# Summing a vector over the partitions: two matmuls replaced by two crossbar turns, in a kernel that TensorE bounds

## The chip, the cores and the metric

One core of one Trainium2 chip. The metric is the device time of one execution in microseconds (us), as the median of several executions. PE is TensorE, DVE is VectorE, ACT is ScalarE, POOL is GpSimd; SP is the queue that issues most of the DMAs.

## The reference, cut to what matters

The program mixes a linear-attention block A and an MLP-mixer block B by a gate. Only the denominator of A matters here:

```python
pq, pk = phi(q), phi(k)                        # [B, H=32, S=2048, Dh=20]
z   = jnp.einsum("bhsd->bhd", pk)              # sum over all 2048 tokens
den = jnp.einsum("bhqd,bhd->bhq", pq, z)[..., None] + 1e-6
o   = num / den
# B: h = gelu(layernorm(x) @ w1); hs = shifted h @ w2; x1 = x + hs
#    b = x1 + gelu(layernorm(x1) @ w3) @ w4
return g * a + (1 - g) * b
```

`z` is one vector of 640 numbers (32 heads of 20). Tokens lie on the 128 partitions, so the sum over tokens has two steps: over the 16 token tiles (elementwise), and over the 128 partitions. Every partition needs the whole vector afterwards, because each multiplies its own `pq` rows with it.

## The kernel before

The first step is a chain of VectorE additions that leaves `zsum` [128, 640] in bf16. The second is the part that changes:

```python
def z_add(t):                                   # VectorE, 15 times; the last writes zsum
    tt(dve, zacc if t < NT - 1 else zsum, pk_tok[:, 0] if t == 1 else zacc, pk_tok[:, t], ALU.add)

def zb_group():                                 # ones^T @ zsum: summed over partitions AND spread to all of them
    b = pair()                                  # two PSUM banks
    mm_group(ps[:, b, 0:512],     [(ones_c[:, 0:128], zsum[:, 0:512])])
    mm_group(ps[:, b + 1, 0:128], [(ones_c[:, 0:128], zsum[:, 512:D])])
    copy(dve, zb[:, :], psf[:, 512 * b:512 * b + D])
...
IT.add("ZB", ("zb",), 0.0, zb_group, deps=[(("z", NT - 1), 1.7), (("w2", 0), 0.0)])

def qn_sum(t):                                  # the reader of zb: VectorE, once for each of 16 tiles
    tt(dve, qprod, pq_tok[:, t + 1], zb, ALU.mult)
    dve(tensor_reduce(dnr[:, 0, sd, :], qprod as 32 heads of 20, ADD))

def t_xn(which, t):                             # "turned tile t": crossbar transpose of a normalised tile, on SP
    sch.dma("sp", xnT[:, :, 128 * t:128 * (t + 1)], xn[:, sx, :], ..., transpose=True)
```

(`...` and shortened arguments mark cuts.) Two facts about the surroundings matter:

- The kernel writes one fixed instruction order for each engine. A small time model inside the program decides that order when the kernel is built; an `IT.add(..., deps=...)` entry is emitted only once its dependencies are done by that model. On the chip each engine works through its list in that order, waiting on semaphores, so a list entry that waits holds up what stands behind it on that engine (turn12_not_held below shows it: VectorE sat idle for 4.74 us before one product, and the W2 sum behind it came 5 us late).
- `xn`, the buffer of normalised tiles, is a ring of three, so tile `t` is normalised only after tile `t - 3` has been turned. Behind the 16 turned tiles of the first norm, SP issues the loads of `w3` and `w4` (2.1 MB each), then the turned tiles of the second norm.

Of the kernel before, what the change touches and what calls it, by code (L numbers as in the profile page):

```python
# [6 lines left out]
F32 = mybir.dt.float32  # L7
ACTF = mybir.ActivationFunctionType
ALU = mybir.AluOpType

S = 2048
D = 640
# [3 lines left out]
NT = S // 128  # L16
NCH = S // 512
KD = D // 128
# [398 lines left out]
def _build(nc, A_x, A_wqkv, A_wo, B_w1, B_w2, B_w3, B_w4, gate_w, out, dbg=None, stop=None):  # L417
    sch = _Sched(nc)
# [37 lines left out]
    pa = Arena(SB_LO, SB_HI - SHARED)  # L456
# [3 lines left out]
    ps = nc.alloc_psum_tensor("ps", [128, 8, 512], F32)  # L460
# [5 lines left out]
    ones_c = pa.alloc("ones_c", [128, 768], BF16)  # L466
# [10 lines left out]
    w2 = pa.alloc("w2", [128, KD, D], BF16)  # L477
# [8 lines left out]
    M_sb = pa.alloc("M_sb", [128, KD, D], BF16)  # L486
    zb = pa.alloc("zb", [128, D], BF16)
    dnr = pa.alloc("dnr", [128, 2, 4, H], F32)
    xn = pa.alloc("xn", [128, 3, D], BF16)
    junk = pa.alloc("junk", [128, 1, D], BF16)  # L490
    qprod = pa.alloc("qprod", [128, D], F32)
    zacc = qprod
    zsum = pa.alloc("zsum", [128, D], BF16)
# [34 lines left out]
    psf = ps[:, :, :].rearrange("p b n -> p (b n)")  # L528
    bank_hold = set()

    def pair():
        best = None
        for k_ in range(4):
            q_ = (bank_rr[0] // 2 + k_) % 4
            tf = 0.0
            ok = True
            for b in (2 * q_, 2 * q_ + 1):
                if b in bank_pend or b in bank_hold:
                    ok = False
                lk = sch.locks.get(b)  # L540
                if lk is not None:
                    tf = max(tf, sch.ev_time.get((lk[1].sem, lk[1].val), 1e18))
            if ok and (best is None or tf < best[0]):
                best = (tf, 2 * q_)
        b = best[1]
        bank_rr[0] = b + 2
        bank_pend.update((b, b + 1))
        return b
# [3 lines left out]
    def slot(name, n):  # L552
        i = slot_ctr.get(name, 0)
        slot_ctr[name] = i + 1
        return i % n

    def nfree(ap):
        n = 1
        for d_ in ap.shape[1:]:
            n *= d_  # L560
        return n

    def in_psum(ap):
        return ap.tensor.name == ps.name

    def act(fn, reads, writes, cost=None):
        if cost is None:
            n = nfree(writes[0])
            cost = max(150.0, 100.0 + 0.833 * n + (70.0 if (reads and in_psum(reads[0])) else 0.0))
            cost += 45.0 * max(0, len(reads) - 1)  # L570
        return sch.op("act", fn, reads, writes, cost=cost)

    def dve(fn, reads, writes, cost=None):
        if cost is None:
            n = nfree(writes[0])
            cost = 65.0 + n / 0.96
        return sch.op("dve", fn, reads, writes, cost=cost)
# [7 lines left out]
    def pe(fn, reads, writes, cost=500.0):  # L585
        for w_ in writes:
            sp_, rl = sch.rects(w_)
            if sp_ == "ps":
                for (_p0, _p1, lo, hi) in rl:
                    for b in range(lo // PS_BANK, (hi - 1) // PS_BANK + 1):  # L590
                        bank_pend.discard(b)
        return sch.op("pe", fn, reads, writes, cost=cost)

    def mm_group(out_ap, pairs, reads_extra=()):
        n = len(pairs)

        def fn(e, out_ap=out_ap, pairs=pairs, n=n):
            ins = None
            for i, (l, r) in enumerate(pairs):
                ins = e.matmul(out_ap, l, r, start=(i == 0), stop=(i == n - 1))  # L600
            return ins
        reads = [a for p in pairs for a in p] + list(reads_extra)
        return pe(fn, reads, [out_ap], cost=n * (max(nfree(pairs[0][1]), 24) * 0.4167 + 2.5))
# [39 lines left out]
    def activation(out_ap, in_ap, func, scale=1.0, bias=0.0, accum=None):  # L643
        rd = [in_ap] + [a for a in (scale, bias) if not isinstance(a, (int, float))]
        wr = [out_ap] + ([accum] if accum is not None else [])
        n = nfree(out_ap)
        cost = max(150.0, 100.0 + 0.833 * n + (70.0 if in_psum(in_ap) else 0.0)) + 45.0 * (len(rd) - 1)
        if accum is not None:
            cost += 91.0
        st_ = ACT_SET.get(func)  # L650
        if st_ is not None and st_ != sch.act_func:
            cost += 1290.0
            sch.act_func = st_
        if accum is not None:
            return act(lambda e: e.activation(out_ap, in_ap, func, bias=bias, scale=scale, accum_out=accum), rd, wr, cost=cost)  # L655
        return act(lambda e: e.activation(out_ap, in_ap, func, bias=bias, scale=scale), rd, wr, cost=cost)  # L656
# [4 lines left out]
    def copy(engf, out_ap, in_ap):  # L661
        cost = None
        if engf is dve and in_ap.dtype == BF16 and out_ap.dtype == BF16:
            cost = 65.0 + nfree(out_ap) / 1.92
        return engf(lambda e: e.tensor_copy(out_ap, in_ap), [in_ap], [out_ap], cost=cost)  # L665
# [90 lines left out]
    def tag_chk(buf, sl, what):  # L756
        assert tags.get((buf, sl)) == what, ("stale ring slot", buf, sl, what, tags.get((buf, sl)))

    IT = _Items()
# [83 lines left out]
    def normalize(which, t, st):  # L843
        sx = slot("xn", 3)
        tag_set("xn", sx, (which, t))
        xn_slots[(which, t)] = sx
        ts(pool, xn[:, sx, :], x_tok[:, t, :], st[:, 6, t:t + 1], st[:, 7, t:t + 1], ALU.mult, ALU.add)

    def t_xn(which, t):
        sx = xn_slots[(which, t)]  # L850
        tag_chk("xn", sx, (which, t))
        sch.dma("sp", xnT[:, :, 128 * t:128 * (t + 1)], xn[:, sx, :], "trn%d" % slot("trn", 4), transpose=True)
# [77 lines left out]
    def stats1(c):  # L930
        ln_chunk_stats(st1, c, lr[:, 4 * c:4 * c + 4, 0:1].rearrange("p t o -> p (t o)"))
        gate_chunk(c)

    for u in range(NT):
        if u % 4 == 0:
            IT.add("S1", ("s1", u // 4), 0.0, lambda u=u: stats1(u // 4), deps=[(("k", u + 3), 1.8)])
        d1 = [(("s1", u // 4), 3.0 + 0.9 * (u % 4))]
        d1.append((("k", 13), 0.0) if u == 0 else (("n1", u - 1), 0.9))
        if u >= 3:
            d1.append((("t1", u - 3), 0.0))  # L940
        IT.add("N1", ("n1", u), 0.0, lambda u=u: normalize(1, u, st1), deps=d1)
        IT.add("T1", ("t1", u), 0.0, lambda u=u: t_xn(1, u), deps=[(("n1", u), 1.1)])
    for u in range(1, NT):
        IT.add("Z", ("z", u), 0.0, lambda u=u: z_add(u), deps=[(("k", NT - 1), 2.0)] if u == 1 else [])
    LAST_EXP = ("k", NT - 1)
# [76 lines left out]
        for j in range(KD):  # L1022
            sch.dma("sp", M_sb[60:68, j, :], Mt[8 * j:8 * j + 8, :], "mt", group_total=KD)

    def zb_group():
        b = pair()
        mm_group(ps[:, b, 0:512], [(ones_c[:, 0:128], zsum[:, 0:512])])
        mm_group(ps[:, b + 1, 0:128], [(ones_c[:, 0:128], zsum[:, 512:D])])
        copy(dve, zb[:, :], psf[:, 512 * b:512 * b + D])

    IT.add("KVF", ("kvt", 1), 0.0, kvt_group, deps=[(("g", KD - 1), 1.0)])
    IT.add("KVF", ("lt", 1), 0.0, lt_evac, deps=[(("kvt", 1), 0.0)])
    IT.add("KVF", ("m", 0), 0.0, m_last, deps=[(("lt", 1), 1.0), (("w1", 2, 2), 0.0)])
    IT.add("KVF", ("m", 1), 0.0, m_first, deps=[(("lt", 1), 1.0), (("w3", 0, 5), 0.0)])
    IT.add("MT", ("mt",), 0.0, m_tail, deps=[(("m", 1), 1.5), (("qt", 2), 0.0)])
    IT.add("ZB", ("zb",), 0.0, zb_group, deps=[(("z", NT - 1), 1.7), (("w2", 0), 0.0)])

    SHIFT = (1, -1, 2, -2)
    PIECES = [[(0, 128, SHIFT[j])] for j in range(4)] + [[(32 * g_, 32 * (g_ + 1), SHIFT[g_]) for g_ in range(4)]]
# [156 lines left out]
    for c in range(NCH):  # L1196
        for j in range(KD):
            deps = [(("t1", u), 0.9) for u in range(4 * c, 4 * c + 4)] if j == 0 else []
# [6 lines left out]
    for t in range(NT):  # L1205
        c = t // 4
        deps = [(("w1", c, KD - 1), GEL)]
# [8 lines left out]
    for u in range(NT):  # L1216
        deps = [(("s2", u // 4), 3.2 + 0.9 * (u % 4))]
# [8 lines left out]
    for c in range(NCH):  # L1226
        for j in range(KFF):
            deps = []
# [4 lines left out]
            if j == 0:  # L1233
                deps = deps0 + [(("t2", u), 0.9) for u in range(4 * c, 4 * c + 4)]
# [11 lines left out]
    for t in range(NT):  # L1246
        deps = [(("zb",), 1.0), (("q", max(t, 2)), 2.0)]
# [12 lines left out]
    for t in range(NT):  # L1260
        c = t // 4
        deps = [(("qt", t), 3.0), (("w4load",), 0.0), (("m", 1), 1.0), (("mt",), 2.5)]
# [29 lines left out]
def bass_gated_mix__linear_attn_block__mixer_s_mlp__prompt_kernel(  # L1292
    nc, A_x, A_wqkv, A_wo, B_x, B_w1, B_w2, B_w3, B_w4, gate_w, out
):
    assert tuple(A_x.shape) == (1, S, D) and tuple(out.shape) == (1, S, D)
    assert tuple(A_wqkv.shape) == (D, 3 * D) and tuple(A_wo.shape) == (D, D)
    assert tuple(B_w1.shape) == (D, D) and tuple(B_w2.shape) == (D, D)
    assert tuple(B_w3.shape) == (D, F) and tuple(B_w4.shape) == (F, D) and tuple(gate_w.shape) == (D,)
    _build(nc, A_x, A_wqkv, A_wo, B_w1, B_w2, B_w3, B_w4, gate_w, out)
# [28 lines left out]
```

## Time and profile before

| what | value | where it is read |
|---|---|---|
| time | 260.59 us (260.18 to 260.70, 3 runs) | run list |
| PE busy | 254.3 of 259.1 us | part 1 of the page |
| chain that ended last | 98% PE | part 4 of the page |
| the two matmuls | 0.27 us | timeline of PE |

Three lines of the page of the kernel before: its first line, PE's line of part 1 (busy us, share, instructions) and the first line of part 4.

```profile
span 259.1 us, 4261 instructions
...
PE 254.3 (98%) x1654; PEld 132.5 (51%) x1685; DVE 152.0 (59%) x288; ACT 106.6 (41%) x216; POOL 93.8 (36%) x151
...
PE 98%; issue 1%; DVE 1%
```

A busy share alone would prove little. The chain says more: followed back from the last instruction, it hardly ever leaves PE. The list of PE's waits from 60 us on says the same: in nearly 200 us PE waits for no other engine.

```profile
engine line waited for: us in total, times, longest us
PE ps L600 <- issue: 0.2, 1, 0.2
PE ps L1167 <- issue: 0.2, 1, 0.2
```

The timeline of PE around the two matmuls (start, length, engine, line, operation, count). A length runs to the modelled end of a pipelined matmul, so lengths overlap; the cost of a group is the distance from its start to the start of the next group.

```profile
82.22 1.24 PE L600 MATMUL ps<-xnT,w 128*128 128x512 bf16 x5
83.30 0.43 PE L600 MATMUL ps<-zsum,ones_c 128*128 128x512 bf16 x2
83.57 1.52 PE L600 MATMUL ps<-w,hsT 128*128 128x512 bf16 x10
```

83.57 - 83.30 = 0.27 us, not the printed 0.43. Another pair of a 512 and a 128 column matmul in the same trace, that of `wq`, has the same distance: one starts at 6.21 us and the next at 6.48 us.

The same stretch on VectorE: the cast that brings `zb` out of PSUM, a W2 sum (L637), then the first product with `zb`.

```profile
82.42 0.82 DVE L637 SCALAR_TENSOR_TENSOR x_tok<-ps,x_tok 128x640 bf16<-128x640 f32 x1 [3.75 <-PE ps L600]
...
83.77 0.82 DVE L665 CAST zb<-ps 128x640 bf16<-128x640 f32 x1 [0.52 <-PE ps L600]
85.13 0.82 DVE L637 SCALAR_TENSOR_TENSOR x_tok<-ps,x_tok 128x640 bf16<-128x640 f32 x1 [0.53 <-PE ps L600]
...
85.88 0.82 DVE L630 TENSOR_TENSOR qprod<-pq_tok,zb 128x640 f32<-128x640 bf16 x1
```

And the SP queue from 72 us on: nine turned tiles with no gap worth naming, the w3 and w4 loads, then, 9 us after the last of those was issued, the first turned tiles of the second norm.

```profile
69.69 13.22 SPq L281 DMA_TRANSPOSE xnT<-xn  x9
82.95 8.14 SPq L285 DMA_DIRECT2D w<-in_B_w_dram  x4
100.15 5.59 SPq L281 DMA_TRANSPOSE xnT<-xn  x4
```

### The profile page before, as it was taken

Reading aid. Unit: us, or ns where it says so; the run is one execution under the profiler, and the core shown is the slowest. Engines: PE = TensorE matmul, PEld = TensorE weight load, DVE = VectorE, ACT = ScalarE, POOL = GpSimd, SP = SyncE. Lnnn points to the kernel's source line nnn. Section 1 sums busy time; section 2 is a strip of 40 time slices with the busy share of each in tenths; the row PEclk is TensorE's granted clock in tenths of the full one; section 3 lists DMA queues with packets and bytes.
Section 4 is the critical chain, followed back from the end, with each engine's and each line's share of the span. In section 5 each row is a group of like instructions: output and inputs, shape, how many; then the busy total and the mean of one; then the engine's idle time right before and its main releaser. Section 6 shows DMA issues by size and latency. Waiting matters only on the chain.

```text
span 259.1 us, 4261 instructions
## 1 busy us (share of the span) xinstructions
PE 254.3 (98%) x1654; PEld 132.5 (51%) x1685; DVE 152.0 (59%) x288; ACT 106.6 (41%) x216; POOL 93.8 (36%) x151
## 2 busy tenths in 40 slices
PE   8999999999999999999999999999999999999996
PEld 4555555544454555554444445554455544455453
DVE  1587877899903799998997407992033410143233
ACT  1496677751365766676854240005500045100000
POOL 4013995969954029666914202320011110021001
DMA  6865998672856992552726640232000020000211
GB/s 181 246 148 137 155 226 156 186 121 50 99 109 124 355 338 47 62 101 52 105 53 122 124 66 0 47 90 67 0 3 0 3 101 0 0 3 1 104 51 51
DMA packets 51406, 25.16 MB, mean 97 GB/s; under 512 B 42766, under 2 KB 49975, under 8 KB 51386
## 3 DMA queue, kind: packets, MB, share of 16 engines
q1 hardware_dynamic: 50000, 21.47, 37.1%
q0 software_dynamic: 1136, 3.28, 5.1%
q8 instruction: 13, 0.21, 0.4%
q10 hardware_dynamic: 250, 0.14, 0.2%
q14 instruction: 7, 0.06, 0.1%
HBM read 12.05 MB, written 2.62 MB: 57 GB/s over the span
## 4 chain that ended last, share of the span: by engine, by line
PE 98%; issue 1%; DVE 1%
PE ps L600 61%; PE ps L1167 22%; PE ps L796 8%; PE ps L889 2%; PE ps L862 1%; PE ps L1079 1%; PE ps L1149 1%; PE ps L890 1%; PE ps L611 1%; DVE x_tok L639 0%; PE ps L969 0%; PE ps L998 0%; DVE xT L665 0%; PE ps L1146 0%
## 5 line engine op out<-in xcount | busy, mean ns | idle before, releaser
L600 PE MATMUL ps<-xnT,w 128*128 128x512 bf16 x348 | 80.4, 379 | 0.7 <-issue 0.2
L1167 PE MATMUL ps<-w,h2T 128*128 128x512 bf16 (+1 forms) x409 | 58.3, 298 | 0.5 <-issue 0.2
L656 ACT ACTIVATE h2T<-ps 128x512 bf16<-128x512 f32 x52 | 30.5, 598 | 67.5 <-PE ps L600 67.5
L600 PEld LDWEIGHTS ps<-xnT,w 128*128 128x128 bf16 x360 | 34.1, 98 | 38.5 <-issue 0.9
L639 DVE SCALAR_TENSOR_TENSOR x_tok<-ps,stg,abx 128x512 bf16<-128x512 f32 (+1 forms) x32 | 17.3, 550 | 61.5 <-PE ps L1167 61.5
L622 POOL TENSOR_SCALAR abx<-x_tok,stg 128x640 f32<-128x640 bf16 x16 | 15.3, 959 | 99.0 <-DVE x_tok L639 94.9
L1167 PEld LDWEIGHTS ps<-w,h2T 128*128 128x128 bf16 x416 | 32.1, 98 | 24.9 <-issue 1.1
L622 POOL TENSOR_SCALAR xn<-x_tok,st 128x640 bf16<-128x640 bf16 x32 | 35.0, 1102 | 14.4 <-DMA xnT<-xn 13.9
L656 ACT ACTIVATE Er<-ps 128x640 bf16<-128x640 f32 x32 | 22.4, 709 | 16.9 <-PE ps L600 8.4
L655 ACT ACTIVATE junk<-x_tok 128x640 bf16<-128x640 bf16 x32 | 23.6, 739 | 3.1 <-DVE x_tok L637 2.6
L656 ACT ACTIVATE hsT<-ps 128x512 bf16<-128x512 f32 (+1 forms) x32 | 18.9, 593 | 13.0 <-PE ps L600 12.7
L600 PE MATMUL ps<-M_sb,pqnT 128*128 128x128 bf16 (+1 forms) x156 | 23.6, 297 | 0.3
L600 PE MATMUL ps<-w,hsT 128*128 128x512 bf16 (+1 forms) x160 | 23.7, 299 | 0.0
L639 DVE SCALAR_TENSOR_TENSOR abx<-ps,stg,abx 128x640 f32<-128x640 f32 x16 | 14.1, 884 | 12.5 <-PE ps L600 11.5
L600 PE MATMUL ps<-wkg,xT 128*128 128x130 bf16 (+1 forms) x138 | 21.1, 298 | 0.1
L600 PE MATMUL ps<-wq,xT 128*128 128x128 bf16 (+1 forms) x128 | 19.7, 298 | 0.1
L600 PEld LDWEIGHTS ps<-w,hsT 128*128 128x128 bf16 x160 | 13.3, 98 | 12.1
L600 PEld LDWEIGHTS ps<-M_sb,pqnT 128*128 128x128 bf16 x160 | 13.2, 98 | 10.8
L796 PE MATMUL ps<-pk_tok,x_tok 128*128 128x512 bf16 x79 | 17.7, 379 | 0.1
L622 DVE TENSOR_SCALAR Er<-Er 128x640 bf16<-128x640 bf16 x32 | 11.8, 368 | 9.4 <-ACT Er L656 9.3
L637 DVE SCALAR_TENSOR_TENSOR x_tok<-ps,x_tok 128x640 bf16<-128x640 f32 x16 | 13.1, 820 | 6.8 <-PE ps L600 5.9
L1108 DVE TENSOR_TENSOR pq_tok<-pq_tok,dnr 128x300 bf16<-128x300 bf16 (+1 forms) x48 | 16.7, 401 | 0.6
(78 smaller groups left out, 228.0 us busy)
## 6 DMA issues: line engine op xcount, KB each, us to landing
w<-in_B_w_dram SPq DMA_DIRECT2D x1, 2160.0 KB, 9.3
w<-in_B_w_dram SPq DMA_DIRECT2D x1, 2080.0 KB, 14.8
out_dram<-x_tok SPq DMA_DIRECT2D x3, 640.0 KB, 3.1
x_tok<-in_A_x_dram SPq DMA_DIRECT2D x2, 640.0 KB, 5.5
w<-in_B_w_dram POOLq DMA_DIRECT2D x8, 160.0 KB, 4.5
x_tok<-in_A_x_dram SPq DMA_DIRECT2D x5, 160.0 KB, 3.0
wq<-in_A_wqkv_dram SPq DMA_DIRECT2D x5, 160.0 KB, 3.9
wkg<-in_A_wqkv_dram SPq DMA_DIRECT2D x5, 160.0 KB, 4.1
```

Of the source, the lines that this page charges most:

```text
L600: ins = e.matmul(out_ap, l, r, start=(i == 0), stop=(i == n - 1))
L611: ins = e.transpose(o, s_, ident[:])
L622: return engf(lambda e: e.tensor_scalar(out_ap, in_ap, s1, s2, op0, op1), rd, [out_ap], cost=cost)
L637: return dve(lambda e: e.scalar_tensor_tensor(out_ap, in0, scalar, in1, op0, op1, accum_out=accum), rd, [out_ap, accum], cost=cost + 70.0)
L639: return dve(lambda e: e.scalar_tensor_tensor(out_ap, in0, scalar, in1, op0, op1), rd, [out_ap], cost=cost)
L655: return act(lambda e: e.activation(out_ap, in_ap, func, bias=bias, scale=scale, accum_out=accum), rd, wr, cost=cost)
L656: return act(lambda e: e.activation(out_ap, in_ap, func, bias=bias, scale=scale), rd, wr, cost=cost)
L796: ins = e.matmul(o, l, r, start=(t0 + q_ == 0), stop=(t0 + q_ == NT - 1))
L862: ins = e.matmul(ps[:, b, 0:n], one[:, 0:128], one[:, 0:n], start=True, stop=True)
L889: e.matmul(ps[:, b, 0:512], l, w[:, k, 0:512], start=(k == 0), stop=(k == KD - 1))
L1108: dve(lambda e, o=o, i0=i0, i1=i1: e.tensor_tensor(o, i0, i1, ALU.mult), [i0, dnr[:, 1, sd, :]], [o], cost=cost)
L1167: ins = e.matmul(o, l, r, start=False, stop=(i == KFF - 1), skip_group_check=(n0 > 0))
```

## The change

Its intent is to take the sum over partitions off PE. A crossbar turn puts the 640 columns of `zsum` on the partitions (five blocks of 128), so VectorE can sum along the free axis. ScalarE spreads each sum over 128 columns, and a second turn brings the vector back, now the same on every partition. So that the second turn is not late, turned tile 12 is held until it is issued.

```diff
+    zc = pa.alloc("zc", [128, KD], F32)
...
-        IT.add("T1", ("t1", u), 0.0, lambda u=u: t_xn(1, u), deps=[(("n1", u), 1.1)])
+        IT.add("T1", ("t1", u), 0.0, lambda u=u: t_xn(1, u), deps=[(("n1", u), 1.1)] + ([(("zb",), 0.0)] if u == 12 else []))
...
-    def zb_group():
-        b = pair()
-        mm_group(ps[:, b, 0:512], [(ones_c[:, 0:128], zsum[:, 0:512])])
-        mm_group(ps[:, b + 1, 0:128], [(ones_c[:, 0:128], zsum[:, 512:D])])
-        copy(dve, zb[:, :], psf[:, 512 * b:512 * b + D])
+    zT = zb[:, :].rearrange("p (k n) -> p k n", n=128)
+    zrep = zsum[:, :].rearrange("p (k n) -> p k n", n=128)
+
+    def z_turn():
+        sch.dma("sp", zT, zsum[:, :], "trz", transpose=True)
+
+    def z_rows():
+        dve(lambda e: e.tensor_reduce(zc[:, :], zT, mybir.AxisListType.X, ALU.add), [zT], [zc[:, :]], cost=820.0)
+        activation(zrep, zc[:, :].unsqueeze(2).to_broadcast([128, KD, 128]), ACTF.Copy)
+
+    def z_back():
+        sch.dma("sp", zT, zsum[:, :], "trz", transpose=True)
...
-    IT.add("ZB", ("zb",), 0.0, zb_group, deps=[(("z", NT - 1), 1.7), (("w2", 0), 0.0)])
+    IT.add("ZB", ("zt",), 0.0, z_turn, deps=[(("z", NT - 1), 1.7), (("t1", 7), 0.0)])
+    IT.add("ZB", ("zr",), 0.0, z_rows, deps=[(("zt",), 2.6), (("kvt", 1), 0.0)])
+    IT.add("ZB", ("zb",), 0.0, z_back, deps=[(("zr",), 1.5)])
```

## The prediction

> **What bounds the kernel now.** TensorE. The page's first part has it 98% busy (254.3 of 259.1 us). The chain that ended last agrees: 98% PE, 1% issue, 1% VectorE. From 70 us on, the list of PE's waits names no other engine, only issue gaps of 0.2 us. So only less PE work, or a new PE wait, moves the time.
>
> **Removed.** Two matmuls (zsum against ones, 512 and 128 columns). In PE's timeline they start at 83.30 and the next group at 83.57 us: 0.27 us, all on the chain. Their PSUM pair and a VectorE cast (0.825 us at 83.77) go too.
>
> **Added.** Two crossbar turns on SP, each as in the trace 1.2-1.3 us of issue and 2.6 us to landing. A VectorE reduction of 640 elements; the one in the trace takes 0.82 us, so VectorE is even. A ScalarE copy, 0.7 us estimated from the 0.70-0.74 us of other 640-element activations; a Copy beside Gelu (M_sb, 125.8 us) needs no table load. [...]
>
> **Moved.**
> - zsum ends at 71.75 us. The first turn goes out beside turned tile 8, at 72-73, landing about 75; tiles 8 to 11 slip 1.3 us. Tile 11 lands about 80.3; its W1 group starts about 86.0: slack over 4 us.
> - Reduction between 75 and 78.5, copy among the gelus about 79-80, way back out about 80, landing about 82.5-83. zb was complete at 84.6, so its first product (85.88) comes at the same time or up to 1.5 us earlier.
> - Turned tile 12 slips from 77.7 to about 81.3; tile 15 waits for xn's ring of three and slips from 81.6 to about 85, landing about 88. Their W1 group starts about 97.3: slack about 9 us.
> - The w3 load slips from 82.95 to about 86.5, landing about 96; first W3 group about 110. The w4 load ends about 3.5 us later, about 102, and may slow the second norm's first turned tiles (issued from 100.15; the fourth lands about 107, needed about 110). It should hold.
> - Gelus about 79-81 slip by up to 0.7 us; PSUM's banks absorb it.
>
> **Sum.** -0.27 us of PE, everything else off the chain: 260.59 - 0.27 = 260.3 us. The order is fixed ahead by the kernel's own model, so a small reorder or other bank assignment can cost or gain a few tenths; before's runs spread 0.5 us. Predicted 260.3 us, range 259.9 to 260.9. Faster by over 2%: 0.01; within 2%: 0.97; slower by over 2%: 0.02.
>
> **What would show it.** Two PE matmuls fewer; PE busy about 0.3 us less between 66 and 100 us; the chain still 98% PE; two more transposes, the second issued about 80 us; zb first read at 84-86 us; tile 15 turned about 85 us.
>
> **What would make it wrong.** (a) A VectorE or ScalarE instruction of the new path placed early in its engine's order and waiting for a turn, so that gelus or W2 sums behind it are late and PE runs out of PSUM banks. (b) The later w4 load colliding with the second norm's turns, so that PE waits at the first W3 group. (c) A changed order of PE groups that exposes another wait, up to about 1 us. (d) An earlier zb or the freed PSUM pair removing gaps; little is to win, as PE has about 0.3 us of them between 70 and 256 us.

## The result, and the profile after

| | before | after |
|---|---|---|
| median of 6 runs | 260.61 us (260.18 to 260.88) | 260.21 us (259.83 to 260.42) |
| ratio | | 0.9987, 95% interval 0.9974 to 0.9999 |

A ratio is the mean time of one kernel's fast runs over that of the other's of the same rounds, so not quite the ratio of the medians. Executions over 1.5% slower than the fastest of the same kernel are left out of the means. The prediction was 260.3 us, range 259.9 to 260.9.

The page of the kernel after, the lines that answer to those above:

```profile
span 259.2 us, 4290 instructions
...
PE 256.2 (99%) x1683; PEld 132.5 (51%) x1683; DVE 151.9 (59%) x288; ACT 107.2 (41%) x217; POOL 93.4 (36%) x151
...
PE 98%; DVE 1%; issue 0%
```

Read carelessly, this page says that nothing was gained: the span grew by 0.1 us, PE is busier and ran more matmuls. None of the three is the work of the change. The trace before has lost matmul records: 1654 stand beside 1685 weight loads, against 1683 beside 1683 in the trace after. The weight loads, 1685 before and 1683 after, show the two that went. The two "issue" waits of the kernel before are likely lost records too: they stand in all five traces that lack about 31 matmul records and in none of the others. The span has another cause. The next two lines are the same matmul of the start-up in PE's timeline, of the kernel before and then of the kernel after:

```profile
5.63 0.38 PE L889 MATMUL ps<-wq,xT 128*128 128x512 bf16 x1
```

```profile
5.69 0.63 PE L890 MATMUL ps<-wq,xT 128*128 128x512 bf16 x1
```

It takes 0.38 us in one and 0.63 us in the other. 0.63 us is what a 512-column matmul takes in turn12_not_held where the granted clock is recorded as 0.50 (four in a row, begun 0.42 us apart, span 1.89 us), so I infer that PE's clock rose later in the execution that was profiled after the change. The clock column of these two traces does not show it: it reads 1.00 from the start in both. Why the two executions differ here is not shown. PE is level in the two traces at 5.4 us and 0.35 us later in the kernel after from 10.8 us to 77 us, so this delay was there before the change had begun.

So the two traces must be compared from a point behind the start-up. I use the place where the chain enters the group that forms kv (line 969 before, 970 after) and the last two VectorE steps, which the chain shows as one piece. From the chain in order of time (start, length, what), before and then after:

```profile
76.62 1.06 PE ps L969 x50
...
256.33 1.08 DVE x_tok L639 x2
```

```profile
76.97 1.06 PE ps L970 x50
...
256.41 1.08 DVE x_tok L640 x2
```

256.33 - 76.62 = 179.71 us before, 256.41 - 76.97 = 179.44 us after: 0.27 us less. I call this number the **fixed stretch**. It is 179.44 us in both traces of the kernel after (the second is the run after_again), while whole runs spread over 0.5 us, so it is the finer instrument. It is still one execution each time, and the kernel before was traced only once.

PE's timeline at the place of the matmuls, after:

```profile
82.57 1.24 PE L601 MATMUL ps<-xnT,w 128*128 128x512 bf16 x5
83.65 1.52 PE L601 MATMUL ps<-w,hsT 128*128 128x512 bf16 x10
```

From group to group it is now 1.08 us (1.35 before). The list of PE's waits from 60 us on is empty. Compared instruction by instruction, PE's order is that of before without the two matmuls. VectorE after:

```profile
77.64 0.82 DVE L1033 TENSOR_REDUCE zc<-zb 128x5 f32<-128x640 bf16 x1 [5.56 <-DMA zb<-zsum]
...
82.77 0.82 DVE L638 SCALAR_TENSOR_TENSOR x_tok<-ps,x_tok 128x640 bf16<-128x640 f32 x1 [3.45 <-PE ps L601]
...
83.52 0.82 DVE L631 TENSOR_TENSOR qprod<-pq_tok,zb 128x640 f32<-128x640 bf16 x1
```

The first product with `zb` now comes directly behind the first W2 sum and ahead of the second, 2.4 us earlier than before. SP after, with the two new turns and the hold:

```profile
74.89 1.27 SPq L281 DMA_TRANSPOSE zb<-zsum  x1
76.21 2.60 SPq L281 DMA_TRANSPOSE xnT<-xn  x2
80.70 1.20 SPq L281 DMA_TRANSPOSE zb<-zsum  x1
81.95 5.58 SPq L281 DMA_TRANSPOSE xnT<-xn  x4
87.57 7.51 SPq L285 DMA_DIRECT2D w<-in_B_w_dram  x4
100.74 5.27 SPq L281 DMA_TRANSPOSE xnT<-xn  x4
```

The queue stands still from 78.8 to 80.7 us (the hold: it waits for ScalarE's copy). The turned tiles 12 to 15 and the w3 and w4 loads go out about 4.5 us later. The second norm's first turns go out 0.6 us later, of which 0.35 us is the start-up.

### The profile page after: what moved, and what is told of

It is laid out like the page before. It is cut to its first block, busy times and chain, and to the rows that moved or that the text cites. A ratio compares the mean times of both kernels' runs of the same rounds, so it can differ in the third digit from the quotient of the medians.

```text
span 259.2 us, 4290 instructions
## 1 busy us (share of the span) xinstructions
PE 256.2 (99%) x1683; PEld 132.5 (51%) x1683; DVE 151.9 (59%) x288; ACT 107.2 (41%) x217; POOL 93.4 (36%) x151
## 4 chain that ended last, share of the span: by engine, by line
PE 98%; DVE 1%; issue 0%
PE ps L601 61%; PE ps L1177 22%; PE ps L797 8%; PE ps L890 2%; PE ps L863 1%; PE ps L1089 1%; PE ps L1159 1%; PE ps L891 1%; PE ps L612 1%; DVE x_tok L640 0%; PE ps L970 0%; PE ps L999 0%; DVE xT L666 0%; PE ps L1156 0%
## 5 line engine op out<-in xcount | busy, mean ns | idle before, releaser
L601 PE MATMUL ps<-xnT,w 128*128 128x512 bf16 x360 | 81.5, 379 | 0.0
L601 PE MATMUL ps<-M_sb,pqnT 128*128 128x512 bf16 (+1 forms) x160 | 24.3, 299 | 0.0
L601 PE MATMUL ps<-wq,xT 128*128 128x512 bf16 (+1 forms) x130 | 19.8, 299 | 0.0
L1118 DVE TENSOR_TENSOR pq_tok<-pq_tok,dnr 128x300 bf16<-128x300 bf16 (+1 forms) x48 | 15.7, 381 | 0.6
L601 PEld LDWEIGHTS ps<-wkg,xT 128*128 128x128 bf16 x140 | 11.4, 97 | 8.4
```

Source lines behind the costliest of these rows:

```text
L601: ins = e.matmul(out_ap, l, r, start=(i == 0), stop=(i == n - 1))
L1118: dve(lambda e, o=o, i0=i0, i1=i1: e.tensor_tensor(o, i0, i1, ALU.mult), [i0, dnr[:, 1, sd, :]], [o], cost=cost)
```

## The experiments

Theory: the gain is PE's own 0.27 us, and everything added lies off the chain. The rivals: the first result was noise; or the gain comes from the earlier `zb`, the missing cast or the freed PSUM pair; or the turns cost something and the removal is worth more. A second question is what the hold on tile 12 is for and how much room there is around it.

The results together; "stretch" is the fixed stretch of the one profiled execution, and "to before" the ratio in the same rounds.

| run | median us (range) | to before (95%) | stretch us |
|---|---|---|---|
| kernel before | 260.33 to 260.61 (medians of its four sets) | 1 | 179.71 |
| kernel after, first result | 260.21 (259.83 to 260.42) | 0.9987 (0.9974 to 0.9999) | 179.44 |
| after_again | 260.52 (260.02 to 260.68) | 0.9993 (0.9981 to 1.0005) | 179.44 |
| turns_and_matmuls | 260.65 (260.12 to 261.09) | 1.0002 (0.9990 to 1.0013) | 179.71 |
| no_matmuls_no_turns | 260.17 (259.70 to 260.68) | 0.9986 (0.9973 to 0.9998) | 179.44 |
| eight_more_pairs | 262.84 (262.62 to 262.95) | 1.0087 (1.0058 to 1.0117) | 181.89 |
| turn12_not_held | 264.80 (264.19 to 266.89) | 1.0168 (1.0142 to 1.0193) | 185.67 |
| hold_tile14 | 260.48 (260.25 to 260.91) | 1.0001 (0.9985 to 1.0017) | 179.65 |
| not_held_late_product | 260.59 (260.39 to 260.69) | 1.0004 (0.9988 to 1.0021) | 179.88 |
| one_dead_turn | 260.29 (259.99 to 260.71) | 0.9993 (0.9978 to 1.0008) | 179.47 |
| two_dead_turns | 262.58 (261.65 to 262.79) | 1.0069 (1.0039 to 1.0099) | 181.31 |
| two_dead_turns_w4_later | 260.16 (259.69 to 260.98) | 0.9990 (0.9968 to 1.0012) | 179.56 |
| five_dead_turns | 273.12 (269.53 to 273.13, its 3 fast runs; a fourth, 273.89, was slow) | 1.0435 (1.0358 to 1.0512) | not taken |

The first four experiments ran on one chip, eight_more_pairs with two_dead_turns and five_dead_turns on a second, the others on a third. All results were correct, except that of no_matmuls_no_turns, which is wrong.

### after_again: is there a gain at all?

No edit.

> The changed kernel itself once more, as the yardstick of this chip. Theory (the gain is the two matmuls taken off TensorE's chain, 0.27 us): about 0.27 us under before, ratio 0.9990. Rival (the first result was noise of the start-up, nothing gained): ratio 1.000.

Measured: ratio 0.9993, and the interval includes 1. The times of this chip alone could not tell 0.27 us from nothing. The fixed stretch could: 179.44 us again. The chain is less steady: on this run's page it is 92% PE and 4% DMA instead of 98% PE, for the same kernel, with the same stretch and again no wait of PE from 60 us on.

### turns_and_matmuls: is it the matmuls?

```diff
+    def dead_pair():
+        b = pair()
+        mm_group(ps[:, b, 0:512], [(ones_c[:, 0:128], w1[:, 0, 0:512])])
+        mm_group(ps[:, b + 1, 0:128], [(ones_c[:, 0:128], w1[:, 0, 512:D])])
...
+    IT.add("DEAD", ("dead",), 0.0, dead_pair, deps=[(("w2", 0), 0.0)])
```

> The changed kernel with a dead pair of matmuls (ones against 512 and 128 columns of a weight, result unread) put back at the old place after the first W2 tile; the turns stay. Theory (only TensorE's own work counts): the gain is gone, level with before, about 260.6 us, ratio 1.000, and 0.27 us over the changed kernel. Rival (the gain is from the earlier zb, from the freed VectorE cast or from the PSUM pair's later eviction): stays at about 260.3, ratio 0.999.

Measured: ratio 1.0002, stretch 179.71 us, that of before to the last digit. The early `zb`, the missing cast and the shorter hold on PSUM are all present here, and nothing is gained. Those rivals fall.

### no_matmuls_no_turns: do the turns cost anything?

```diff
 # on the kernel before; wrong result on purpose
-        b = pair()
-        mm_group(...)
-        mm_group(...)
-        copy(dve, zb[:, :], psf[:, 512 * b:512 * b + D])
+        dve(lambda e: e.tensor_copy(zb[:, :], zsum[:, :]), [zsum[:, :]], [zb[:, :]], cost=731.0)
```

> The kernel before with the two matmuls dropped and zb copied by VectorE straight from zsum: wrong result on purpose, no turns at all. TensorE's order is that of the changed kernel. Theory (the turns cost nothing): as fast as the changed kernel, 0.27 us under before, ratio 0.999, difference to the changed kernel under 0.1 us. Rival (the removal is worth more and the turns give part of it back): 0.2 us or more faster than the changed kernel.

Measured: 260.17 us, stretch 179.44 us, the same as the kernel after. The turns, the reduction and the copy cost nothing as they are placed. The changed kernel has the whole of what removing the two matmuls can give.

### eight_more_pairs: is the price right?

```diff
 # on the kernel before
         copy(dve, zb[:, :], psf[:, 512 * b:512 * b + D])
+        for _ in range(8):
+            b = pair()
+            mm_group(ps[:, b, 0:512], [(ones_c[:, 0:128], zsum[:, 0:512])])
+            mm_group(ps[:, b + 1, 0:128], [(ones_c[:, 0:128], zsum[:, 512:D])])
```

> The kernel before with eight more pairs of the same matmuls (ones against zsum, result unread) right after the first. Theory (a pair is worth 0.27 us because TensorE waits for nothing from 70 us on): 8 x 0.27 = 2.2 us over before, about 262.8 us, ratio 1.0083. Rival (some of PE's work there hides in gaps): under half of that.

Measured: ratio 1.0087, about 2.3 us; the stretch grew by 181.89 - 179.71 = 2.18 us, which is 0.2725 us a pair. PE's work here converts to time one for one.

### turn12_not_held: what is the hold for?

```diff
-        IT.add("T1", ("t1", u), ..., deps=[(("n1", u), 1.1)] + ([(("zb",), 0.0)] if u == 12 else []))
+        IT.add("T1", ("t1", u), ..., deps=[(("n1", u), 1.1)])
```

The orders of PE, DVE, ACT and POOL are those of the kernel after; only on SP does the way back now stand behind tile 15.

> The changed kernel without the hold on turned tile 12: on SP the way back then stands behind turned tile 15; TensorE, VectorE, ScalarE and GpSimd have the same order. The way back goes out about 84 instead of 80.7 us and zb lands about 87 instead of 83.3. VectorE is 97% busy from 84 to 100 us and takes the zb product before the next W2 sum, so about 3.5 us of lateness run through it into the second norm: the fourth turned tile of the second norm lands about 110.8 instead of 107.3, and the first W3 group is due at 109.6. Theory: slower than the changed kernel by about 1 us (0.3 to 2.5), with a new wait of PE about 85-112 us. Rival (there is slack enough, the hold is idle): within 0.2 us of the changed kernel.

Measured: 264.80 us, 4.3 us over after_again on the same chip. The direction is as expected, but the size is four times my central guess and outside my range. SP and then VectorE of this run:

```profile
84.10 1.28 SPq L281 DMA_TRANSPOSE zb<-zsum  x1
85.42 8.87 SPq L285 DMA_DIRECT2D w<-in_B_w_dram  x4
```

```profile
83.01 0.82 DVE L638 SCALAR_TENSOR_TENSOR x_tok<-ps,x_tok 128x640 bf16<-128x640 f32 x1 [3.74 <-PE ps L601]
...
88.58 0.82 DVE L631 TENSOR_TENSOR qprod<-pq_tok,zb 128x640 f32<-128x640 bf16 x1 [4.74 <-DMA zb<-zsum]
...
90.18 0.81 DVE L638 SCALAR_TENSOR_TENSOR x_tok<-ps,x_tok 128x640 bf16<-128x640 f32 x1
```

The bracket reads: VectorE sat idle for 4.74 us before the product, waiting for the turn of `zb`. The way back went out 3.4 us later than with the hold, and it took 4.46 us to land instead of 2.6 us. Why it landed slowly is not shown: the w3 load was issued right behind it, but in the kernel after turned tile 13, issued at 83.27 us, took 4.22 us as well, and there no load was issued before 87.57 us. The second W2 sum, which PE's PSUM banks wait for, stands behind that product: it came at 90.18 instead of 85.21 us. PE's waits in the same run:

```profile
PE ps L601 <- DVE x_tok L638: 1.9, 1, 1.9
PE ps L999 <- ACT hsT L657: 1.2, 1, 1.2
PE ps L601 <- DVE dnr L623: 1.1, 1, 1.1
```

Together they are 4.2 us. VectorE had little room to catch up, because it is nearly full there. The busy time of each engine from 84 to 100 us (PE, PEld, DVE, ACT, POOL, granted clock, DMA share, GB/s), first of the kernel after, then without the hold:

```profile
84.00:100.00 16.00, 16.00 (x102) 8.08 (x100) 15.57 (x40) 12.15 (x25) 3.99 (x9) 1.00 0.94 286
```

```profile
84.00:100.00 16.00, 11.76 (x71) 5.53 (x69) 11.14 (x28) 7.97 (x16) 0.20 (x1) 0.96 1.01 293
```

In the kernel after, VectorE is busy for 15.57 of 16 us. There was also a second loss. In two of the six runs, the profiled one among them, the mean granted clock was 0.994 and the time 266.6 to 266.9 us; in the other four it was 1.000 and 264.2 to 264.9 us. In the profiled run the clock was at half (0.50) from 98.7 to 102 us, after PE's gaps. Compared with the kernel after, weight load by weight load, PE was 4.5 us late when the clock fell and 6.2 us late when it was back. So of the 6.2 us that the stretch is longer, 4.5 us come from the waits and 1.7 us from the half clock.

### not_held_late_product: is it VectorE's order?

The same as turn12_not_held, with one more dependency for the first product:

```diff
-        deps = [(("zb",), 1.0), (("q", max(t, 2)), 2.0)]
+        deps = [(("zb",), 1.0), (("q", max(t, 2)), 2.0)] + ([(("w2", 2), 0.0)] if t == 0 else [])
```

This puts three W2 sums ahead of the first product. It also changes the order of VectorE, ScalarE and GpSimd in a few later places; PE's stays.

> The changed kernel without the hold, and with the first product with zb put behind the third W2 sum in VectorE's order, so that the late zb (about 88.5 us) stops no W2 sum. Theory (the 4.3 us came from VectorE standing at that product with the W2 sums behind it): all but 0.5 us of it comes back, about 260.3 to 260.8 us. Rival (the later w3 load or the changed order of the turns cost it): stays at 263 us or more.

Measured: 260.59 us, stretch 179.88 us, 0.44 us over the kernel after. With the way back about as late as in turn12_not_held (issued at 83.90 us) nearly the whole loss is gone. What remains sits at two places where PE waited for ScalarE, whose order this edit changed too: 0.16 us at 94.6 us and 0.28 us at 125.1 us. The first product now follows the third sum without a wait:

```profile
88.24 0.82 DVE L638 SCALAR_TENSOR_TENSOR x_tok<-ps,x_tok 128x640 bf16<-128x640 f32 x1 [2.68 <-PE ps L601]
...
88.99 0.82 DVE L631 TENSOR_TENSOR qprod<-pq_tok,zb 128x640 f32<-128x640 bf16 x1
```

So nearly all the harm of a late `zb` comes from what stands behind its first reader.

### hold_tile14: does the place of the hold matter?

```diff
-  ... + ([(("zb",), 0.0)] if u == 12 else []))
+  ... + ([(("zb",), 0.0)] if u == 14 else []))
```

> The changed kernel with turned tile 14 held instead of tile 12, so the way back stands on SP behind tile 13; every other engine's order is the same. The way back goes out about 82 instead of 80.7 us and zb lands about 84.8 instead of 83.3. Theory (a late zb stops VectorE at its first product and every us of that lateness reaches PE, as without the hold: zb 5.2 us later by landing, 4.3 us lost): VectorE loses about 1.3 us before the W2 sums; part of it is taken up by PSUM, 0 to 1.3 us over the changed kernel. Rival (only the landing next to the w3 load hurts, not the place among the turns): within 0.2 us of the changed kernel, because here two turns still stand between the way back and the w3 load.

Measured: ratio 1.0001, stretch 179.65 us, 0.21 us over the kernel after. The expectation was built on a `zb` that lands 1.5 us later, and that did not happen: the two tiles let ahead take 2.6 us of SP, of which 1.9 us is time in which SP otherwise stands still. Counted from the start of the fixed stretch the way back went out only 0.6 us later, and VectorE waited 0.4 us for it. The time alone does not separate 0.21 us from the rival's "within 0.2 us". The traces do. The way back landed in 2.67 us, so its landing was not slow; VectorE was about 0.4 us late from the first product on and did not make it up in 10 us; and PE runs level with the kernel after up to 93.7 us, where it falls 0.21 us behind all at once, at a W1 group that waited for a W2 sum (L638). That is the path of the theory. It also shows how narrow the hold's margin is: in the kernel after `zb` lands at 83.31 us and its first product starts at 83.52 us, so a `zb` 0.7 us later is already felt.

### one_dead_turn, two_dead_turns, five_dead_turns: how much room is there?

```diff
     def z_back():
         sch.dma("sp", zT, zsum[:, :], "trz", transpose=True)
+        for i in range(N):      # N = 1, 2, 5; the result is never read; hidden from the kernel's time model
+            sch.dma("sp", junkT, zsum[:, :], "trj%d" % i, transpose=True)
```

No engine's order changes but SP's, which gets N entries more.

> The changed kernel with two dead turns on SP between the way back and turned tile 12, each waiting for the one before it to land (2.7 us each), so that tiles 12 to 15 and the w3 and w4 loads slip by about 5.4 us; no engine's order changes. Theory (slack about 9 us at the W1 group of tiles 12 to 15, which lands at 88.5 and starts at 97.4 us): the time of the changed kernel, within 0.3 us. Rival (the slip of the w4 load already collides with the second norm's turns from 100.7 us on): slower by 0.5 us or more, with PE waiting at the first W3 group about 109.6 us.

Measured: 262.58 us, stretch +1.87 us. My reading of the slack was wrong and the rival right. The W1 group that I had given 9 us did not wait; PE's only waits from 60 us on in this run are these, the first of them at the first W3 group:

```profile
PE ps L602 <- DMA xnT<-xn: 1.3, 1, 1.3
PE ps L602 <- DVE x_tok L639: 0.3, 1, 0.3
```

The turned tiles of the second norm that this group needs are in SP's view of that tile from 101 to 113 us:

```profile
L281 SPq DMA_TRANSPOSE xnT<-xn x4: 1201/1442/2366, 101.8 to 109.3; - x4
...
DMA to landing us min/median/max: 2.6/5.9/6.5
```

They landed after 5.9 us in the median instead of 2.6 us, since the w4 load was still running, and as `xn` is a ring of three the fourth could not be normalised before the first had landed; it went out at 109.3 us instead of 104.7 us. This wait makes up 1.47 of the 1.87 us. By a comparison of the weight loads with the kernel after, the other 0.40 us arose earlier, at 94.8 us, where PE waited for a W2 sum. In this execution a small VectorE instruction ahead of that sum had taken 0.75 us instead of 0.18 us (at 90.3 us); why, the trace does not show.

> The changed kernel with one dead turn behind the way back: tiles 12 to 15 and the w3 and w4 loads slip by 1.3 us. Two dead turns cost 2.2 us because the w4 load ran into the first turned tile of the second norm (landing 6.5 instead of 2.6 us). Theory (in the changed kernel the w4 load ends about 101.7 us, that turn goes out at 100.7, so there is about 1 to 3 us left): 0 to 0.7 us over the changed kernel. Rival (the changed kernel stands at the edge already): 1 us or more.

Measured: ratio 0.9993, stretch 179.47 us, 0.03 us over. One dead turn is free and two are not. The edge is near: with one, the loads slipped by 2.7 us and not by the 1.3 us that I had expected, and the first three turns of the second norm already took 4.0 us in the median to land (2.6 us in the kernel after), but PE did not wait for them.

> The same with five dead turns, a slip of about 13.5 us, beyond the slack. Theory: turned tile 15 lands about 102 us, so the W1 group due at 97.4 us waits about 4.6 us; the w4 issue then holds SP until about 108, so the second norm's turns come late too: 4 to 7 us over the changed kernel, with PE's wait named at those turns. If the time moved by under 1 us, my reading of the slack would be wrong.

Measured: 273.12 us in the median of the fast runs, 12.8 us over the kernel before of the same rounds (11.3 us by the ratio of the means), about twice what I expected. PE waits 8.3 us for the two sets of turned tiles, and the granted clock falls twice to half speed behind those gaps (0.50 from 102 to 104 us and from 120 to 122 us), which I had not counted.

### two_dead_turns_w4_later: is it the w4 load?

```diff
-    IT.add("MISC", ("w4load",), 0.0, w4_load, deps=[(("kvt", 1), 0.0), (("t1", NT - 1), 0.0), (("z", NT - 1), 1.5)])
+    IT.add("MISC", ("w4load",), 0.0, w4_load, deps=[(("kvt", 1), 0.0), (("t2", 3), 0.0), (("z", NT - 1), 1.5)])
```

> The two dead turns again, but the w4 load issued behind the fourth turned tile of the second norm, so that it cannot run into the first four. Theory (the 2.2 us came from that collision): back to within 0.4 us of the changed kernel, and no PE wait at the first W3 group; the next four turns may land late but are due only about 125 us. Rival (the slip of tiles 12 to 15 itself cost it): stays about 2 us over.

Measured: 260.16 us, stretch 179.56 us. About the same slip of tiles 12 to 15 now costs 0.12 us; the first four turns land in 2.6 us in the median again, as in the kernel after, and PE waits at no W3 group. What had cost the 1.47 us was the w4 load beside the second norm's turns, not the delay of the first norm's tiles. The 0.40 us at the W2 sum did not recur here, before the w4 load had any part in it, so this run does not explain it.

No run beat the kernel after by more than the noise, and none of them points to one that would: its PE waits for nothing from 60 us to the end, and no_matmuls_no_turns, which does without the turns altogether, is no faster.

## Why the prediction was right

- **The size, -0.27 us: right.** The stretch shortened by 0.27 us; putting the pair back restored it exactly, and eight more pairs cost 8 x 0.2725 us.
- **Everything else off the chain: right, as placed.** no_matmuls_no_turns shows that turns, reduction and copy cost nothing.
- **Costs of the added operations: right.** Turns 1.2 to 1.3 us of issue and 2.6 to 2.7 us to landing, reduction 0.82 us, copy 0.73 us against an estimate of 0.7. The copy brought no table load: ScalarE has two in each trace, at 1.85 and 68.42 us before and at 1.85 and 68.77 us after. VectorE's busy time is 151.9 against 152.0 us. One sign that the prediction named can't be read: PE's busy time between 66 and 100 us, which should have fallen by 0.3 us, is 33.68 us before and 34.00 us after, since the trace before lost records of matmuls.
- **Where the first turn stands: off.** I placed it at 72 to 73 us beside tile 8. It went out at 74.89 us behind tile 9, as the kernel's model emits it later than the data allow.
- **When zb is first read: off.** I said 84 to 86 us; it was 83.52. I had assumed the old order on VectorE, with the second W2 sum first. The kernel's model, seeing `zb` earlier, put the product ahead of that sum. In this run it did no harm, but it made VectorE's order depend on the turn, and turn12_not_held shows the price.
- **The slacks: one right and beside the point.** "Slack about 9 us" for tile 15 may well hold, as that group did not wait with two dead turns. The slack that binds is that of the w4 load against the second norm's turns. I had named that danger (b) without sizing it: it lies between one dead turn and two. Counted from the start of the fixed stretch, the w3 load and with it the w4 load went out 2.7 us later with one and 4.6 us later with two.
- **What the hold is worth: not asked.** I costed it as a delay of tiles 12 to 15 and never asked what happens without it. Danger (a) names the mechanism, W2 sums stuck on VectorE behind an instruction that waits for a turn, but I did not see that the hold is what keeps it away. That the prediction came true although I had the order on VectorE wrong is in part luck: `zb` landed 0.2 us before its reader was due. The hold is worth 4.3 us, sixteen times the gain. Without it the change would have made the kernel 1.7% slower.

## What to carry to other kernels

When PE is the whole chain and waits for nothing, as here, a piece of PE work is worth its start-to-start distance in the timeline (0.27 us here; eight_more_pairs gave 0.2725 us a pair), and a replacement on idle engines is worth it only if every queue it passes through has room for it; look first at what stands *behind* each new waiting instruction on its engine, since that is what paid here (4.3 us in turn12_not_held, nearly all of it back in not_held_late_product). Against a spread of 0.5 us, a gain of 0.3 us is best read from a stretch between two fixed instructions behind the start-up, and made sure by putting the removed work back. Check the place of the bulk loads against the next small transfers that something waits for: in two_dead_turns the three turns that went out while the w4 load was running took 5.6 to 6.5 us to land instead of 2.6 us, and PE waited 1.3 us at the tile they fill.

## What the runs measured of the matmuls, the clock and the turns

- The pair of a 512 and a 128 column matmul takes 0.2725 us from start to start (eight_more_pairs), in a stream in which each matmul has its own weight load. A W1 group of five 512-column matmuls, each with its own weight load, takes 1.08 us, 216 ns each.
- In five_dead_turns the granted clock was at half (0.50) behind waits of PE of 3.5 and 4.8 us, and in two_dead_turns, with no wait over 1.3 us from 60 us on, it stayed at 1.00. In turn12_not_held no single wait was longer than 1.9 us, but the last two (1.2 and 1.9 us) had only 0.46 us of six small matmuls between them, 3.57 us in all from 95.10 to 98.67 us, and the clock was at half from 98.7 to 102 us. It fell in two of the six runs (mean granted clock 0.994, 2 us longer); the other four had 1.000. Why it fell in these executions and not in the others is not shown.
- The 32 turns of 128x640 bf16 `xn` tiles in the kernel before took 1.2 us of issue and 2.6 us to landing in the median, 2.5 and 4.8 us at most. The three that went out beside a running 2.1 MB load in two_dead_turns took 5.6 to 6.5 us to land. Turns issued a little before the loads were slower in some runs: 4.2 us in the kernel after (issued at 83.27 us), 4.46 us in turn12_not_held (84.10 us) and 3.8 us in not_held_late_product (83.90 us), with a load right behind it in the last two and none in the first; the cause is not shown.
